# Weight transfers from ScalarE's queue, decay rows inside SBUF and two other edits at the start of an attention and two-layer feed-forward kernel

## The chip, the core and the metric

The kernel runs on one core of a Trainium2 chip. The metric is the device time of one execution in microseconds (us), the median of three runs. Engines are called as in the profile: PE (TensorE matmul), PEld (TensorE weight load), DVE (VectorE), ACT (ScalarE), POOL (GpSimd), SP (SyncE, which here only issues DMAs).

## What is computed

Causal attention with a forget-gate decay, then two feed-forward layers on the same 2304 tokens. Cut to its core:

```python
# batch 4, heads 8, seq 576, head_dim 64
scores  = q @ k.T / sqrt(64)
cum     = cumsum(log(clip(f, 1e-4, 1)))          # per batch and head
scores  = where(causal, -1e9, scores + cum[i] - cum[j])
attn    = softmax(scores)
x       = attn @ v                               # 2304 x 512
h = x @ w_in;  x = (h * tanh(softplus(h))) @ w_out            # d_ff 2048
x = (sigmoid(x @ w_gate) * (x @ w_val)) @ w_out2              # d_ff 1536
```

## The kernel before

**Stages.** Attention runs per batch (b = 0 to 3) and pair of heads (p = 0 to 3), in chunks of 128 query rows: chunks 0 and 1 are the first part of a batch, chunks 2, 3 and 4 the second. The first feed-forward layer works on blocks of 256 tokens (`h_ps`, then `y_ps`), eight groups g of 256 hidden units each; the second layer (`bank`, `o_acc`) follows. Each matrix is held as a sum of two float16 parts, so each product takes three matmuls. Attention of batches 1 to 3 is interleaved with the first layer; batch 0's first part has nothing beside it and opens the program.

**The order.** The kernel writes its instructions through a list scheduler of its own, the class `Order`. Every step is a task that yields an engine and an estimated duration (`yield "DVE", t_dve(512), "port"`); the scheduler keeps a clock for each engine and picks by due time and by readiness. The word "port" (or engine POOL) makes a step take a common clock that it keeps for DVE and POOL. `pick` chooses the engine of a step by the estimates. The estimates therefore decide both the order on each engine and who does what; on the chip each engine then runs its own list in that order, waiting on semaphores. Where `Order` sees PE idle for over 0.6 us it calls `fill`, which issues matmuls on the mask into the open accumulator before its first real use, or as products with zeros: work with no result (lines with `y_ps<-mask`, L1069).

**The start.** `decay` (L439) loads the gates `f` into `ft`, clips them (DVE, L447), takes the logarithm with its sum (ACT, L449), adds the carries of the four segments by a matmul (PE, L455, `carry_ps`) and scans (DVE, L460) into `cum`. `cum` is written to the DRAM scratch `cum_f` (L463), and from there `first_rows` (L525) brings it back as one row of `Q32` and one of `K32` (L533: keys rq, rk for the first 256 positions, rk2 for the rest). `Q32` (tile `sab`) and `K32` (tile `mab`) hold q and k in float32 with two more rows, so that one matmul gives scores plus decay; the constant rows are set on POOL by `ones` (L402). `prep_first` loads q and k (L544, L546).

**The first softmax.** `scores_first` (L734) makes two score tiles for chunks 0 and 1 of a pair (L741, `s_ps`), then in the same task, one after the other, the masked minimum on DVE (L698, helper `softmax_part`) and the exponential on ACT (L764); then the transposes by matmul (L788, `t_ps`), and `pv` multiplies with v (L952, `o_ps`).

**Weights.** `load_w` brings a weight piece of 512 KB as 64-bit numbers (L655, raw tile `xt`), turns it into float32 by three DVE steps (`float32`, L632, L636, L640) and splits it (`scaled` L495 on ACT, L498 on DVE; `rest` L514 on DVE, or L519 on ACT and L523 on POOL). Three raw buffers and two float32 buffers are in turn use. The first piece was held until the last q and k transfer was issued, the second until rk had landed; all are issued from SP. w_in needs 16 pieces and w_out 16.

Of the kernel before, what the change touches and what calls it, by code (L numbers as in the profile page):

```python
# [295 lines left out]

def t_dve2(cols):
    return cols * 0.52e-3 + 0.066
# [11 lines left out]
def attention_moe_moe_kernel(ctx, tc, qk, v, f, carry, ident, rows_q, rows_k, w_in, w_out, w_gate, w_val, w_out2, out):  # L310
# [121 lines left out]
    def decay():  # L432
        ft = words(xt[0], 1280, 2 * SL).bitcast(FP32)
        cum = words(xt[0], 1280 + 2 * SL, 2 * SL).bitcast(FP32)
# [26 lines left out]
        for seg in range(4):  # L461
            yield "SP", 0.5, 5000, ("cum_f", seg)
            nc.sync.dma_start(out=cum_f[:, seg * SL:(seg + 1) * SL], in_=cum[seg * NH:seg * NH + 2 * NPB])  # L463
            if seg == 1:
                spawn(first_rows(), -50)
                od.due(-20)
        yield from need(*[("cum_f", seg) for seg in range(4)])
# [32 lines left out]
    def rest(dst, a, scale, b, n, pool=False):  # L500
# [3 lines left out]
        plans = [[("DVE", t_dve(n), "port")]]  # L504
# [20 lines left out]
    def first_rows():  # L525
        yield from need("ones", ("cum_f", 0), ("cum_f", 1))
        for key, row, n in (("rq", Q32[64:65], 256), ("rk", K32[65:KF], 256), ("rk2", K32[65:KF], S)):
            c0 = 256 if key == "rk2" else 0
            if c0:
                od.due(-20)  # L530
                yield from need(("cum_f", 2), ("cum_f", 3))
            yield "SP", 0.5, 10000, key
            nc.sync.dma_start(  # L533
                out=row.rearrange("o a q s -> o (a q) s")[:, :, c0:n], in_=cum_f[:, c0:n].unsqueeze(0)
            )

    def prep_first(p, part, turn):
# [10 lines left out]
        if part:  # L548
            yield from need(("cum_f", 2), ("cum_f", 3))
# [5 lines left out]
        yield from need(*(("rk2", ("rq2", p)) if part else ("rq", "rk")))  # L555
# [47 lines left out]
    def prep_v(b, p, turn):  # L603
        i = b * NPB + p
        if b == 0:
            yield from need("rk")
# [14 lines left out]
        yield from scaled(t[:, :, 0, :], s, S_V, 640)  # L621
        yield from rest(t[:, :, 1, :], s, S_V, t[:, :, 0, :], 640, b < VPOOL)
# [7 lines left out]
    def float32(w, raw):  # L630
        yield "DVE", 0.335, "port"
# [3 lines left out]
        yield "DVE", 0.6, "port"  # L635
# [3 lines left out]
        yield "DVE", 0.6, "port"  # L639
# [4 lines left out]
    def load_w(hi, lo, src, scale, key, n):  # L644

        yield from need(*(((("st", NPB - 1),),) + (("rk",),) * n)[n])
# [5 lines left out]
        if n < NFIRST:  # L652
            od.due(-26.5)
# [277 lines left out]
    def pv(b, p, part, dues, turn):  # L931
# [41 lines left out]
        if cs[-1] == 4:  # L973
            give("vt", vi)
# [671 lines left out]
```

## Time and profile before

| | |
|---|---|
| median of 3 runs | 940.15 us (939.47 to 943.29) |
| the profiled execution | 940.69 us |
| its span, first to last instruction | 938.8 us |
| around the span | 1.89 us |
| mean granted TensorE clock | 0.987 |

PE is busy for 97% of the span, but a part of that is work on the mask, and a part runs at a lower clock. The views used below are the page's first two parts (busy time by engine, and the span in 40 slices), the table of windows (busy time of each engine in stretches of the span), the timeline of the first 25 us, and the timelines of POOL and DVE around 92 us.

### The profile page before, as it was taken

What the parts mean: (1) busy time and instruction counts of PE and PEld (TensorE: products, weight loads), DVE (VectorE), ACT (ScalarE), POOL (GpSimd) and SP (SyncE); (2) the same over time, 40 slices, a digit from 0 to 9 for tenths busy, and PEclk for the clock granted to TensorE, in tenths of its full rate; (3) what the DMA queues carried; (4) which work ended last, traced back from release to release, by engine and by line L of the source; (5) the groups of instructions that cost most, each with busy time, mean ns of one, the idle gap of its engine ahead of it and who ended that gap; (6) DMA issues with size and microseconds to landing.
All of it is one profiled execution on the core that took longest, in us unless ns stands there. A gap on an engine that the chain in (4) does not pass through costs nothing.

```text
span 938.8 us, 21014 instructions
## 1 busy us (share of the span) xinstructions
PE 910.6 (97%) x8619; PEld 718.0 (76%) x8619; DVE 589.6 (63%) x1348; ACT 559.5 (60%) x1097; POOL 84.6 (9%) x80
## 2 busy tenths in 40 slices
PE   6998999999999999999999999999999999999998
PEld 5656688778888888788888877777777777777786
DVE  5779989875765746666699999954136232432333
ACT  4788769888888878788444465544324332432343
POOL 3022302020111001000200010200000000000000
PEclk9879899999999999999999999999999999999999
DMA  6487997667465565635334443101000000100000
GB/s 194 125 208 196 226 229 198 142 128 150 113 141 117 110 148 107 124 66 93 100 121 151 157 134 115 45 6 41 1 1 23 24 1 1 45 1 1 12 36 23
DMA packets 145405, 90.47 MB, mean 96 GB/s; under 512 B 103599, under 2 KB 127119, under 8 KB 145310
## 3 DMA queue, kind: packets, MB, share of 16 engines
q1 hardware_dynamic: 145310, 89.15, 39.1%
q8 instruction: 67, 1.10, 0.5%
q14 instruction: 28, 0.23, 0.1%
HBM read 50.78 MB, written 4.85 MB: 59 GB/s over the span
## 4 chain that ended last, share of the span: by engine, by line
PE 42%; DVE 12%; DMA 2%; issue 1%; ACT 1%; POOL 1%; POOLq 0%; DVEq 0%; ACTq 0%
PE bank L1342 7%; PE bank L1343 7%; PE bank L1344 7%; PE o_acc L1490 4%; PE o_acc L1489 4%; PE o_acc L1488 4%; DVE wf L636 2%; DVE wf L640 2%; DMA wraw<-w_val 1%; DVE wf L632 1%; PE y_ps L1104 1%; PE o_ps L964 1%; DMA wraw<-w_gate 1%; DVE g L1027 1%; PE h_ps L1054 1%
## 5 line engine op out<-in xcount | busy, mean ns | idle before, releaser
L1054 PE MATMUL h_ps<-xt,win 128*128 128x256 f16 x576 | 158.2, 275 | 2.1 <-DVE g L1027 2.1
L1056 PE MATMUL h_ps<-xt,win 128*128 128x256 f16 x576 | 157.7, 274 | 2.3 <-POOL win L523 1.9
L1104 PE MATMUL y_ps<-g,wout 128*128 128x256 f16 x576 | 158.1, 274 | 0.1
L1055 PE MATMUL h_ps<-xt,win 128*128 128x256 f16 x576 | 157.8, 274 | 0.0
L1106 PE MATMUL y_ps<-g,wout 128*128 128x256 f16 x576 | 157.7, 274 | 0.0
L1105 PE MATMUL y_ps<-g,wout 128*128 128x256 f16 x576 | 157.7, 274 | 0.0
L1432 DVE TENSOR_TENSOR v<-bank,e 128x512 f32<-128x512 f32 (+1 forms) x30 | 19.1, 637 | 167.8 <-ACT bank L1349 167.8
L1349 ACT ACTIVATE bank<-bank 128x512 f32<-128x512 f32 (+1 forms) x90 | 48.5, 539 | 90.7 <-PE bank L1344 88.7
L514 DVE SCALAR_TENSOR_TENSOR pp<-sp,sm,pp 128x384 f16<-128x384 f32 (+4 forms) x120 | 77.7, 659 | 20.4 <-ACT pp L495 18.7
L698 DVE CUSTOM_DVE_ANT_0 sp<-s_ps,mask 128x384 f32<-128x384 f32 (+4 forms) x144 | 67.4, 492 | 30.3 <-PE s_ps L832 28.2
L495 ACT ACTIVATE pp<-sp,sm 128x384 f16<-128x384 f32 (+4 forms) x115 | 67.8, 606 | 9.9 <-issue 3.4
L847 ACT ACTIVATE sp<-sp,sm 128x384 f32<-128x384 f32 (+3 forms) x112 | 63.6, 569 | 13.3 <-DVE sm L698 12.5
L1054 PEld LDWEIGHTS <-win 128*128 128x128 f16 x576 | 56.6, 98 | 14.8 <-issue 3.2
L1055 PEld LDWEIGHTS <-win 128*128 128x128 f16 x576 | 56.7, 98 | 13.7 <-issue 5.1
L1104 PEld LDWEIGHTS <-wout 128*128 128x128 f16 x576 | 56.6, 98 | 11.0 <-ACT sp L910 0.9
L1056 PEld LDWEIGHTS <-win 128*128 128x128 f16 x576 | 56.6, 98 | 10.1 <-POOL win L523 2.2
L1105 PEld LDWEIGHTS <-wout 128*128 128x128 f16 x576 | 56.7, 98 | 7.8 <-issue 0.3
L1106 PEld LDWEIGHTS <-wout 128*128 128x128 f16 x576 | 56.6, 98 | 6.8
L1027 DVE SCALAR_TENSOR_TENSOR g<-h_ps,g 128x512 f16<-128x512 f32 x72 | 48.9, 684 | 19.1 <-ACT g L1023 18.8
L964 PEld LDWEIGHTS <-vt 128*64 128x64 f16 x1368 | 36.3, 112 | 15.2 <-issue 11.4
L1017 ACT ACTIVATE h_ps<-h_ps 128x512 f32<-128x512 f32 x72 | 41.7, 585 | 10.1 <-PE h_ps L1056 9.6
L964 PE MATMUL o_ps<-pt,vt 128*64 128x128 f16 (+1 forms) x1368 | 44.3, 216 | 2.7 <-DMA pt<-pp 1.6
(206 smaller groups left out, 2289.4 us busy)
## 6 DMA issues: line engine op xcount, KB each, us to landing
xt<-w_in SPq DMA_DIRECT2D x16, 512.0 KB
xt<-w_out SPq DMA_DIRECT2D x16, 512.0 KB
wraw<-w_gate SPq DMA_DIRECT2D x12, 512.0 KB
wraw<-w_val SPq DMA_DIRECT2D x12, 512.0 KB
wraw<-w_out SPq DMA_DIRECT2D x12, 512.0 KB
out<-ob SPq DMA_DIRECT2D x18, 256.0 KB
vst<-v SPq DMA_DIRECT2D x12, 320.0 KB
st<-qk SPq DMA_DIRECT2D x12, 320.0 KB
```

The costliest lines, as they stand in the source:

```text
L495: nc.scalar.activation(out=dst, in_=src, func=ACTF.Copy, scale=scale, bias=bias)
L514: nc.vector.scalar_tensor_tensor(dst, a, scale, b, op0=ALU.mult, op1=ALU.subtract)
L698: nc.vector.tensor_tensor_reduce(out=sp, in0=ps_ap, in1=mk, op0=ALU.add, op1=ALU.min, scale=-0.125, scalar=1.0e38, accum_out=mn,)
L964: nc.tensor.matmul(o_ps[64 * hh:64 * hh + 64, col:col + n], lhsT=vv[:, jc, vl, 64 * hh:64 * hh + 64], rhs=ptt[:, k, q0:q0 + n], start=(jc ...
L1054: nc.tensor.matmul(dst, lhsT=wh, rhs=xh, start=(k == 0), stop=False)
L1055: nc.tensor.matmul(dst, lhsT=wh, rhs=xl, start=False, stop=False)
L1056: nc.tensor.matmul(dst, lhsT=wl, rhs=xh, start=False, stop=(k == KD - 1))
L1104: nc.tensor.matmul(dst, lhsT=wh, rhs=gh, start=first, stop=False, skip_group_check=True)
L1105: nc.tensor.matmul(dst, lhsT=wl, rhs=gh, start=False, stop=False, skip_group_check=True)
L1106: nc.tensor.matmul(dst, lhsT=wh, rhs=gl, start=False, stop=last, skip_group_check=True)
L1342: nc.tensor.matmul(dst, lhsT=wh, rhs=xh[:, k], start=first, stop=False, skip_group_check=True)
L1343: nc.tensor.matmul(dst, lhsT=wh, rhs=xl[:, k], start=False, stop=False, skip_group_check=True)
```

## The change

The change does six things.

1. The first two weight pieces are issued from ACT's queue, the first before anything else there, the second when pair 0's q and k have been asked for (`NFIRST` = 2). All others stay on SP.
2. The constant rows of `Q32` and `K32` come by two DMAs from a new input `const`; the two POOL memsets go.
3. `cum` and `ft` lie in other tiles (`wout`), and the rows rq and rk go directly from `cum` in SBUF to their places, as two DMAs each; only segments 1 to 3 still go to `cum_f`, for the second part.
4. In `scores_first` the softmax of each chunk is a task of its own, `soft`, spawned as soon as its score tile is done, instead of a loop after both.
5. The estimates of DVE steps marked "port" become 0.049 us longer (`t_dvep`), those in `float32` 0.04 to 0.055 us.
6. The low part of v for batch 0 waits for that batch's last product (`("pv", i)`).

```diff
+def t_dvep(cols):
+    return cols * 1.04e-3 + 0.115
...
     def ones():
-        yield "POOL", 2.5
-        nc.gpsimd.memset(K32[64:KF], 8.0)
-        yield "POOL", 1.5
-        nc.gpsimd.memset(Q32[64:KF], -8.0)
+        yield "SP", 0.5, 10000, "ones_k"
+        nc.sync.dma_start(out=K32[64:65].rearrange("o a q s -> o (a q s)"), in_=const[0:1])
+        yield "SP", 0.5, 10000, "ones_q"
+        nc.sync.dma_start(
+            out=Q32[65:KF].rearrange("o a q s -> o (a q s)"), in_=const[1:2, 0:2 * NPB * 320]
+        )
+        yield from need("ones_k", "ones_q")
...
-        ft = words(xt[0], 1280, 2 * SL).bitcast(FP32)
-        cum = words(xt[0], 1280 + 2 * SL, 2 * SL).bitcast(FP32)
+        ft = words(wout[NG1 - 1], 1536, 2 * SL).bitcast(FP32)
+        cum = words(wout[NG1 - 2], 1536, 2 * SL).bitcast(FP32)
...
-        for seg in range(4):
+        for row, key in ((Q32[64:65], "rq"), (K32[65:KF], "rk")):
+            for seg in range(2):
+                n = min(SL, 256 - seg * SL)
+                yield "SP", 0.5, 10000, (key, seg)
+                nc.sync.dma_start(
+                    out=row.rearrange("o a q s -> o (a q) s")[:, :, seg * SL:seg * SL + n],
+                    in_=cum[seg * NH:seg * NH + 2 * NPB, 0:n],
+                )
+        od.due(-20)
+        for seg in range(1, 4):
...
-        plans = [[("DVE", t_dve(n), "port")]]
+        plans = [[("DVE", t_dvep(n), "port")]]
...
         yield from scaled(t[:, :, 0, :], s, S_V, 640)
+        if b == 0:
+            yield from need(("pv", i))
...
-        yield "DVE", 0.335, "port"
+        yield "DVE", 0.39, "port"
...
-        yield "DVE", 0.6, "port"
+        yield "DVE", 0.64, "port"
...
-        yield from need(*(((("st", NPB - 1),),) + (("rk",),) * n)[n])
+        if n:
+            yield from need(("st", 0) if n < NFIRST else ("rk", 1))
...
-            od.due(-26.5)
+            od.due(-40 + 9.9 * n)
         yield "SP", 0.5, 128 * 4096
-        nc.sync.dma_start(
+        (nc.scalar if n < NFIRST else nc.sync).dma_start(
...
+        def soft(gi, pst, tag, si):
+            c, n = gi, (gi + 1) * 128
+            yield from need("mask")
+            yield "DVE", 2 * t_dve(n)
+            for hh in range(2):
+                k = 2 * gi + hh
+                softmax_part(
+                    pst[:, hh * n:hh * n + n], mask[:, 512 - 128 * c:640], sps[k][1], sm[:, k:k + 1],
+                )
+            give(tag, si)
+            yield "ACT", 2 * t_act(n, 0.28), "exp"
...
-            banks.append((pst, tag, si))
+            spawn(soft(gi, pst, tag, si), od.cur["due"])
         give("q", qi)
-        for gi in range(2):
...
+        yield from need(("soft", p, 0), ("soft", p, 1))
         yield from weigh(sm, 4)
```

The new lines shift the line numbers: L632, L636 and L640 become L645, L649 and L653; L698 becomes L712; L455 becomes L462; L655 becomes L669.

**First place: the issuing queues at the start of the program.** SP before, from the second transfer on (`carry` and `ident` are constants; `mab` and `sab` are K32 and Q32):

```order
L442 DMA wout_84<-carry 128x128
L544 DMA mab<-qk 64x2x256
L546 DMA sab<-qk 64x2x256
L397 DMA win_83<-ident 128x128
...
L463 DMA cum_f<-xt_71 8x144 x2
L546 DMA sab<-qk 64x2x256
L544 DMA mab<-qk 64x2x256
L546 DMA sab<-qk 64x2x256
L533 DMA sab<-cum_f 1x8x256
L533 DMA mab<-cum_f 1x8x256
L655 DMA xt_74<-w_in 128x2x512
```

SP after, from the same transfer on (`wout_90` is `cum`):

```order
L449 DMA wout_84<-carry 128x128
L409 DMA mab<-const 1x4608
L411 DMA sab<-const 1x2560
L554 DMA mab<-qk 64x2x256
L556 DMA sab<-qk 64x2x256
L401 DMA win_83<-ident 128x128
L473 DMA sab<-wout_90 1x8x144
L473 DMA sab<-wout_90 1x8x112
L473 DMA mab<-wout_90 1x8x144
L473 DMA mab<-wout_90 1x8x112
L554 DMA mab<-qk 64x2x256
```

ACT after, its first rows (before, the queue began with the table load and held no transfer):

```order
L669 DMA xt_74<-w_in 128x2x512
L456 ACT_TABLE_LOAD
L456 ACTIVATE wout_91,wout_84<-wout_91 128x144
L457 ACT_TABLE_LOAD
L457 ACTIVATE wout_84<-wout_84 128x1
L669 DMA xt_73<-w_in 128x2x512
L510 ACTIVATE win_76<-xt_75 128x512
L763 ACTIVATE wout_88,sm<-wout_88,sm 128x128 x2
```

The rows of rq and rk now leave SP directly behind pair 0's q and k and ident, ahead of the q and k of pairs 1 to 3, and two weight transfers stand on ACT. With the semaphores shown, ident waits for the semaphore that the first weight transfer raises, and the transfer behind the four rows (pair 1's k) for that of the second.

**Second place: DVE, from the carry to the first softmax.** Before (`carry_ps` is the carry, `wout_88` pair 0's scores):

```order
L457 COPY wout_84<-carry_ps 128x1
L460 SCALAR_TENSOR_TENSOR xt_71<-xt_71,wout_84 128x144
L419 MEMSET mask_93 128x144
L420 COPY mask_93<-mask 64x64
...
L698 ISA wout_88,sm<-s_ps,mask 128x128
L698 ISA sm 128x1
...
L632 TENSOR_SCALAR xt_75<-xt_74 128x512
L471 CAST win_82<-xt_71 128x144
```

After:

```order
L464 COPY wout_84<-carry_ps 128x1
L467 SCALAR_TENSOR_TENSOR wout_90<-wout_91,wout_84 128x144
L645 TENSOR_SCALAR xt_75<-xt_74 128x512
L649 SCALAR_TENSOR_TENSOR xt_75<-xt_74,xt_75 128x512
L653 SCALAR_TENSOR_TENSOR xt_75<-xt_74,xt_75 128x512
L529 SCALAR_TENSOR_TENSOR win_76<-xt_75,win_76 128x512
L645 TENSOR_SCALAR xt_75<-xt_73 128x512
L649 SCALAR_TENSOR_TENSOR xt_75<-xt_73,xt_75 128x512
L712 ISA wout_88,sm<-s_ps,mask 128x128
```

Six steps of weight conversion moved from behind the first softmax to ahead of it. On PE, 18 of the mask matmuls now stand ahead of the carry and 14 between it and the first scores, where 35 stood behind the carry; in the whole program there are 138 of them, and 143 before. The engines' shares move too: POOL has 22 more two-input steps (`TENSOR_TENSOR`) than before.

## Rows read from the trace of the kernel before

**Rows 1.** The page's first two parts: busy us by engine; TensorE's granted clock, 40 slices.

```profile
PE 910.6 (97%) x8619; PEld 718.0 (76%) x8619; DVE 589.6 (63%) x1348; ACT 559.5 (60%) x1097; POOL 84.6 (9%) x80
PEclk9879899999999999999999999999999999999999
```

**Rows 2.** Windows: stretch, its us, busy us (and count) of each engine, PEclk, DMA, GB/s.

```profile
10.00:20.00 10.00, 7.41 (x52) 5.79 (x49) 5.70 (x29) 3.88 (x16) 0.00 (x0) 1.00 0.82 265
20.00:30.00 10.00, 9.31 (x43) 7.04 (x44) 8.37 (x31) 8.51 (x33) 0.00 (x0) 0.66 1.01 245
...
40.00:50.00 10.00, 9.46 (x59) 6.45 (x60) 9.90 (x30) 7.96 (x18) 0.44 (x1) 1.00 0.45 90
...
60.00:70.00 10.00, 10.00 (x65) 5.81 (x64) 8.35 (x23) 6.41 (x14) 0.00 (x0) 0.52 0.61 152
70.00:80.00 10.00, 9.09 (x72) 6.09 (x70) 9.86 (x23) 9.94 (x19) 0.69 (x1) 0.97 0.66 162
80.00:100.00 20.00, 16.30 (x152) 11.70 (x151) 19.68 (x46) 14.27 (x25) 5.44 (x6) 0.86 0.89 213
...
200.00:300.00 100.00, 100.00 (x1149) 83.80 (x1147) 64.61 (x193) 85.03 (x169) 12.60 (x13) 1.00 0.62 132
...
500.00:600.00 100.00, 98.70 (x826) 80.61 (x825) 92.70 (x157) 51.91 (x89) 10.81 (x6) 1.00 0.40 129
```

**Rows 3.** Timeline, 0 to 13 us: start, us, engine, line, step [idle before, releaser].

```profile
0.73 3.93 POOL L405 MEMSET mab<- 2x4608 f32 x1 [0.29 <-POOLq L1636]
2.67 2.08 DVE L447 TENSOR_SCALAR xt<-xt 128x144 f32<-128x144 f32 x1 [1.65 <-DMA xt<-f]
4.79 0.32 ACT L449 ACTIVATE xt<-xt 128x144 f32<-128x144 f32 x1 [2.78 <-DVE xt L447]
5.26 0.59 PE L455 MATMUL carry_ps<-wout 128*128 128x1 f32 x2 [5.26 <-ACT xt L449]
5.71 5.63 PE L1069 MATMUL y_ps<-mask 128*128 128x256 bf16 x35
6.15 0.52 DVE L460 TENSOR_TENSOR_SCAN xt<-xt,wout 128x144 f32<-128x144 f32 x1
6.70 0.67 SPq L463 DMA_DIRECT2D cum_f<-xt  x2
10.19 0.63 SPq L533 DMA_DIRECT2D mab<-cum_f  x1
12.35 1.55 PE L741 MATMUL s_ps<-mab,sab 66*128 66x128 f32 x8 [1.01 <-DMA mab<-cum_f]
```

**Rows 4.** Timeline, 5 to 25 us: table load, first weight piece, its steps, a softmax.

```profile
5.22 1.28 ACT L450 ACT_TABLE_LOAD   x1
10.86 0.45 SPq L655 DMA_DIRECT2D xt<-w_in  x1
13.06 0.29 DVE L698 CUSTOM_DVE_ANT_0 wout<-s_ps,mask 128x128 f32<-128x128 f32 x1 [4.66 <-PE s_ps L741]
14.60 0.43 DVE L632 TENSOR_SCALAR xt<-xt 128x512 int32<-128x512 int32 x1 [1.02 <-DMA xt<-w_in]
18.14 0.69 DVE L640 SCALAR_TENSOR_TENSOR xt<-xt,xt 128x512 int32<-128x512 int32 x1
```

**Rows 5.** PE's timeline, 30 to 110 us: first layer's first matmul, two longest waits.

```profile
41.51 0.27 PE L1054 MATMUL h_ps<-xt,win 128*128 128x256 f16 x1
...
58.88 0.28 PE L1056 MATMUL h_ps<-xt,win 128*128 128x256 f16 x1 [1.89 <-POOL win L523]
...
95.85 2.19 PE L894 MATMUL s_ps<-mab,sab 66*64 66x288 f32 x8 [2.71 <-DVE sm L698]
```

**Rows 6.** POOL's timeline, then DVE's, around 92 us.

```profile
92.03 1.30 POOL L523 TENSOR_TENSOR pp<-sp,pp 128x512 f16<-128x512 f32 x1 [6.96 <-ACT sp L519]
92.24 1.65 DVE L636 SCALAR_TENSOR_TENSOR xt<-xt,xt 128x512 int32<-128x512 int32 x1
98.17 0.67 DVE L636 SCALAR_TENSOR_TENSOR xt<-xt,xt 128x512 int32<-128x512 int32 x1
```

More of the change, by code (lines that the diff above doesn't have):

```diff
@@ L460, in decay @@
         nc.vector.tensor_tensor_scan(out=cum, data0=ft, data1=zt, initial=car, op0=ALU.add, op1=ALU.add)
-        for seg in range(4):
+        for row, key in ((Q32[64:65], "rq"), (K32[65:KF], "rk")):
[8 more added lines that the diff above has]
+        for seg in range(1, 4):
             yield "SP", 0.5, 5000, ("cum_f", seg)
             nc.sync.dma_start(out=cum_f[:, seg * SL:(seg + 1) * SL], in_=cum[seg * NH:seg * NH + 2 * NPB])
[L464 to L467, printed above, removed]
+        spawn(first_rows(), -20)
+        yield from need(*[("cum_f", seg) for seg in range(1, 4)])
         od.due(0)
@@ L525, in first_rows @@
     def first_rows():
[L526 to L532, printed above, removed]
-            nc.sync.dma_start(
-                out=row.rearrange("o a q s -> o (a q) s")[:, :, c0:n], in_=cum_f[:, c0:n].unsqueeze(0)
-            )
+        yield from need(*[("cum_f", seg) for seg in range(1, 4)])
+        yield "SP", 0.5, 10000, "rk2"
+        nc.sync.dma_start(
+            out=K32[65:KF].rearrange("o a q s -> o (a q) s")[:, :, 256:S], in_=cum_f[:, 256:S].unsqueeze(0)
+        )
     def prep_first(p, part, turn):
@@ L548, in prep_first @@
         if part:
-            yield from need(("cum_f", 2), ("cum_f", 3))
+            yield from need(*[("cum_f", seg) for seg in range(1, 4)])
             yield "SP", 0.5, 10000, ("rq2", p)
@@ L554, in prep_first @@
         yield from need(("k32", p, part), ("q32", p, part))
-        yield from need(*(("rk2", ("rq2", p)) if part else ("rq", "rk")))
+        first = [(k, seg) for k in ("rq", "rk") for seg in range(2)]
+        yield from need("ones", *(("rk2", ("rq2", p)) if part else first))
         done(("q", p, part))
@@ L605, in prep_v @@
         if b == 0:
-            yield from need("rk")
+            yield from need(("rk", 1))
             (vi,) = yield from take("vt", turn=turn)
@@ L638, in float32 @@
         )
-        yield "DVE", 0.6, "port"
+        yield "DVE", 0.64, "port"
         nc.vector.scalar_tensor_tensor(
@@ L974, in pv @@
             give("vt", vi)
+        done(("pv", i))
         t0 = b * S + cs[0] * 128
@@ L1158, in add @@
     def add(out, a, b, op, n):
-        (plan,) = pick([("DVE", t_dve(n), "port")], [("POOL", t_pool(n))])
+        (plan,) = pick([("DVE", t_dvep(n), "port")], [("POOL", t_pool(n))])
         yield plan
@@ L1260, in mixed @@
     def mixed(out, v, other):
-        yield "DVE", t_dve(512), "port"
+        yield "DVE", t_dvep(512), "port"
         nc.vector.scalar_tensor_tensor(out, v, S_VL / S_GT, other, op0=ALU.mult, op1=ALU.subtract)
@@ L1322, in s_pair @@
         yield from scaled(dst[:, 0], a, 1.0, n, pool=False)
-        yield "DVE", t_dve(n), "port"
+        yield "DVE", t_dvep(n), "port"
         nc.vector.tensor_tensor(dst[:, 1], a, dst[:, 0], op=ALU.subtract)
```

40 lines of the change are left out of this document (14 added, 26 removed).

## The prediction

> **What bounds the kernel now.** I read the page's busy times first: PE is busy for 97% of the span [rows 1]. The matmuls that count are the same in both kernels, so the time can only change through what else fills PE: waits, mask matmuls, and stretches at the lower clock. The windows then show where these are [rows 2]. From 200 us on PE is full at clock 1.00 and DVE has a third of its time free; there the end is set by PE's work alone, and a microsecond won before it arrives at the end. Before 100 us DVE is full: 9.90 of 10 us from 40 on, 9.86 of 10 from 70, 19.68 of 20 from 80, while PE waits for it; the longest wait there, 2.71 us, ends on a DVE step [rows 5]. Only from 10 to 20 us does DVE stand idle for long, 5.70 of 10 [rows 2]; before its first softmax at 13.06 it sat idle for 4.66 us [rows 4]. So the change is worth what it gives DVE earlier: work in the idle time at the start, or less work before 100 us.
>
> The start is one chain [rows 3]: gates land at 2.67, clip until 4.75, logarithm, carry at 5.26, scan until 6.67, row to DRAM at 6.70, row back until its wait ends at 12.35 with the first scores.
>
> **The change part by part.** The sum is made against the profiled execution, 940.69 us with a span of 938.8; it lies 0.54 above the median of 940.15, which I take off at the end.
>
> *Clip and carry.* The clip took 2.08 us for 144 columns and ended when the POOL memset that began at 0.73 for 3.93 us ended, at 4.66 [rows 3]. A one-input step of 512 columns takes 0.43 [rows 4], so without the memset the clip should take some 0.23 (my estimate from that row, scaled down with a fixed part): 1.85 us less. But the mask matmuls that now stand ahead of the carry take part of it back. 35 took 5.63 us, 0.161 each [rows 3], so 18 take 2.9 us. They need the mask memset, which now opens POOL at 0.73 and, with 640 columns at the old memset's 3.93 / 4608 us each, should be done by about 1.4; PE reaches the carry at 4.3 to 4.5 instead of 5.26. The carry to the scan's end took 6.67 - 5.26 = 1.41 us. The scan ends at about 5.8: **0.9 us** won, between 0.3 (mask matmuls at a lower clock, or gates late) and 1.8 (none of that).
>
> *Two hops become one.* From the scan's end to the first scores went 12.35 - 6.67 = 5.68 us: a write to DRAM, its landing, two row reads, their landing. The read of rk was issued at 10.19 and let PE go at 12.35, so issue and landing of one such transfer take 2.16 us [rows 3]. Now four transfers follow each other on SP; the two small writes took 0.67 together, a row read 0.63 [rows 3]. The last is issued 1.0 to 1.9 us after the scan and lands 2.16 later: 3.2 to 4.1 us in place of 5.68. How long a move inside SBUF from eight partitions into one takes is not in this trace; the nearest row is the read of rk, and I take it. Won **2.0 us** (1.6 to 2.5; nothing, if such a move needs what both hops did). The constant rows are cheap to issue, two transfers of some 0.6 ahead of pair 0's q and k, and finished long before the scan. First scores near 9.4 in place of 12.35, a gain of **2.9 us** from these two items.
>
> *Weights from ACT.* The issue of one takes 0.45, and 14.60 - 10.86 = 3.74 us pass until DVE can begin on it [rows 4]. The first now goes at 0.73 and is there at about 4.5, before the scan ends; the second waits for the logarithm and a table load of 1.28 [rows 4], goes at about 5 and lands near 9. On ACT the two issues delay nothing that is not waiting anyway: the logarithm waited for the clip for 2.78 us [rows 3]. Three steps and the low part of the first piece, and two steps of the second, cost DVE some 0.43 + 0.69 + 0.69 + 0.69 + 0.43 + 0.69 = 3.6 us (0.43 for a one-input step, 0.69 for a two-input one) [rows 4]. Before, they ran from 14.60 on, between the softmaxes, now from 5.8 to about 10, in time that was idle. They do not give 3.6 at the end: before 38 us DVE waits for other things too. Counting through DVE's list to the fourth pair's attention result (the fourth step on `xt<-o_ps`), one piece more has been turned into float32 than before: 0.43 + 2 x 0.69 = 1.8 us of work that DVE need not do when it is full. Half of it I count as arriving, **0.9 us** (0 to 1.8).
>
> From 10 to 20 us, where the first weight pieces moved before, the DMA engines were busy for 0.82 of the time at 265 GB/s [rows 2]; from 0.7 to 5 us, gates, carry and pair 0's q and k will now move beside 512 KB. The page "DMA: Bandwidth & Descriptors" of the Trainium skill (section "Issuing engines are not separate DMA queues") speaks against the edit: transfers issued from several engines run on the same 16 DMA engines and interleave, so that another queue saves only the time of issuing. By it ACT's queue would be worth two issues of 0.45, and the gates would land later. The gain counted above comes from the earlier date and not from the queue, and the gates may be 0.8 us late before the 18 mask matmuls no longer hide it.
>
> *A task per chunk.* The first chunk's softmax may run and free its score bank before the second is scored. DVE's work per pair is the same, and DVE is what PE waits for there, so I count nothing; at best a wait of PE for a bank goes, and the mask matmuls or the next wait for DVE take its place.
>
> *Estimates and the order.* Longer "port" steps make the scheduler move work off DVE. Counted step by step with the durations of the trace, DVE has some 3 us less to do by the first layer's tenth step, and ACT some 3 more, with 9.94 of 10 us busy from 70 on [rows 2]. And 22 more two-input steps go to POOL. One such step of 1.30 us at 92.03 made a DVE step that began at 92.24 take 1.65 instead of 0.67 [rows 6], so each may cost DVE up to 0.98. Some four of them fall before 100 us. I take **0.7 us** won (from 3 won to 4 lost).
>
> *Mask matmuls.* 138 for 143. A matmul of the span takes 910.6 / 8619 = 0.106 us in the mean [rows 1], 5 of them **0.5 us**.
>
> *The v task and the new `cum_f` order.* The second part's rows come from segments 1 to 3 to DRAM and back as before, now behind the transfers of v, and the second part's scores stand behind all first scores on PE, which cover it. Nothing, or 1 us lost if those scores come so early that the rows are late.
>
> Sum: 2.9 + 0.9 + 0.7 + 0.5 = 5.0. The profiled execution would take 935.7, the median **935.2 us**.
>
> **The rivals.**
>
> *A. The start is held by the second weight transfer.* DVE's list now has two steps of the second piece ahead of the first softmax. If that piece lands late, all softmaxes are queued behind it, and PE and ACT wait for them. It goes from ACT only after the logarithm and a table load, and pair 1's k waits on SP for the same landing. It would have to land at 12 instead of 9 for the first softmax to come at 13.1 as before. Then the 2.9 is lost and the rest stays: 940.15 - 0.9 - 0.7 - 0.5 = 938.0. For it: 512 KB from 0.73 on have company. Against: the 3.74 us were measured in a stretch with 265 GB/s of other traffic and weights together [rows 2].
>
> *B. Lower clock goes with the waits.* From 20 to 30 us the granted clock was 0.66 and from 60 to 70 it was 0.52, that is mostly the lower of the two levels (1.2 of 2.4 GHz); the second fell after PE's wait of 1.89 us that ended at 58.88, a wait for POOL's part of a weight piece [rows 2, 5]. A stretch like that costs 10 x 0.48 = 4.8 us of matmul time. If the earlier weights remove this wait, about as much again is won: 930.4. Against: such waits come from POOL's late steps, and POOL gets more of them; and PE now idles from the last of the 14 mask matmuls, near 7, to 9.4, which may lower the clock at the first scores.
>
> *C. POOL takes DVE's time: slower.* The 22 added POOL steps at up to 0.98 us make up to 21.6 us of DVE time [rows 6]. After 200 us DVE has room, except from 500 to 600, where it is busy for 92.70 of 100 [rows 2] and where four of the added steps lie in the second layer's weights. From ten hits at places where PE waits for DVE, the forecast's gain is used up and 4.8 more is lost: 935.2 + 9.8 = 945.0. The page "SBUF — State Buffer" of the Trainium skill (section "Who interferes with whom") says that a vector step with two SBUF inputs contends with a GpSimd step that reads SBUF and that the later one blocks fully; the trace agrees with 1.65 against 0.67, and by that rule no part of a hit is softened. Against C: most hits fall where PE has other work queued.
>
> **How the numbers follow.** Chances: forecast 0.48 (932.5 to 938), A 0.22, B 0.18, C 0.12. "Faster" means below 935.45, 0.5% under 940.15, about what a measurement can tell from no change. Of the forecast's 0.48 some 0.28 lie below it; with B that is 0.46. The rest of the forecast and A give 0.42 for no change, C gives 0.12 for slower. The forecast lies close to that border, which is why both are near even. For 8 in 10 the range takes the forecast, A and half of B, with the nearer part of C: 930.0 to 943.5.
>
> **What would show it.** The clip takes under 0.4 us and the scan ends near 5.8; if it ends after 6.5, the carry item is wrong. The first scores begin between 8.5 and 10.3; later means that the rows inside SBUF or rival A decide, told apart by what ended PE's or DVE's wait. DVE converts from 6 to 10 us, and its first softmax stands near 10. The first `h_ps` matmul comes at 37 to 38 in place of 41.51 [rows 5]. From 200 us on PE should be full as before; if the gap to the kernel before changes there, C or chance in the order decides. A granted clock of 1.00 from 60 to 70 speaks for B, DVE steps of 1.3 us and more beside POOL steps for C.

## The result and the profile after

The changed kernel takes **950.08 us** (median, 949.41 to 952.25) against 941.64 of the kernel before in the same session: a ratio of 1.0101, 95% interval 1.0079 to 1.0122. I had forecast 935.2 with 930.0 to 943.5; it became slower, by 1.0%. The profiled execution after took 952.25 us with a span of 950.5.

The page's busy times and granted clock of the changed kernel, beside [rows 1]:

```profile
PE 918.9 (97%) x8614; PEld 721.4 (76%) x8614; DVE 590.7 (62%) x1324; ACT 571.1 (60%) x1116; POOL 101.8 (11%) x100
PEclk7979999989989999999999999999999999999999
```

ACT has 11.6 us more and POOL 17.2 more, as expected of the estimates, but DVE is not relieved, with 24 instructions fewer. Its start on the timeline, beside [rows 3] and [rows 4] (start, us, engine, line, step, and in brackets the idle time before and what ended it):

```profile
1.42 3.84 PE L1084 MATMUL y_ps<-mask 128*128 128x256 bf16 x18 [1.42 <-POOL mask L419]
3.62 0.23 DVE L454 TENSOR_SCALAR wout<-wout 128x144 f32<-128x144 f32 x1 [1.23 <-DMA wout<-f]
4.12 0.19 ACT L456 ACTIVATION_READ_ACCUMULATOR wout<-wout 128x1 f32 x1
5.36 0.35 PE L462 MATMUL carry_ps<-wout 128*128 128x1 f32 x2
5.58 1.69 PE L1084 MATMUL y_ps<-mask 128*128 128x256 bf16 x14
6.01 0.52 DVE L467 TENSOR_TENSOR_SCAN wout<-wout,wout 128x144 f32<-128x144 f32 x1
9.96 1.35 PE L776 MATMUL s_ps<-mab,sab 66*128 66x128 f32 x6 [2.69 <-issue]
10.68 0.29 DVE L712 CUSTOM_DVE_ANT_0 wout<-s_ps,mask 128x128 f32<-128x128 f32 x1
38.12 0.27 PE L1069 MATMUL h_ps<-xt,win 128*128 128x256 f16 x1
```

The mask matmuls have two paces. In the kernel before the first 16 follow each other every 0.213 us and the rest every 0.109; the changed kernel has its first 16 at the slow pace too (before in two stretches that share a matmul, then after):

```profile
5.71 3.55 PE L1069 MATMUL y_ps<-mask 128*128 128x256 bf16 x16
8.86 2.47 PE L1069 MATMUL y_ps<-mask 128*128 128x256 bf16 x20
1.42 3.60 PE L1084 MATMUL y_ps<-mask 128*128 128x256 bf16 x16 [1.42 <-POOL mask L419]
```

The first scores come 2.39 us earlier, the first layer's first matmul 3.39 us earlier (41.51 before). Then the windows of the changed kernel, beside [rows 2] (stretch, its length, busy us and count of PE, PEld, DVE, ACT, POOL, then granted clock, DMA share, GB/s):

```profile
0.00:100.00 100.00, 86.85 (x640) 61.43 (x640) 75.54 (x204) 72.59 (x164) 14.72 (x18) 0.86 0.68 181
...
10.00:20.00 10.00, 8.64 (x31) 6.41 (x31) 5.63 (x29) 6.25 (x25) 0.91 (x1) 0.59 0.78 226
...
60.00:70.00 10.00, 7.66 (x51) 4.62 (x49) 7.67 (x20) 7.54 (x14) 1.07 (x1) 0.66 0.68 180
...
180.00:190.00 10.00, 3.65 (x21) 1.67 (x19) 8.50 (x25) 6.54 (x16) 1.55 (x2) 0.79 0.62 123
190.00:200.00 10.00, 8.00 (x76) 4.92 (x76) 5.59 (x17) 7.62 (x17) 2.60 (x3) 0.53 0.69 143
200.00:300.00 100.00, 96.60 (x1079) 80.06 (x1078) 60.45 (x178) 81.09 (x162) 13.79 (x14) 0.97 0.61 118
```

and the same of the kernel before, which its rows ahead did not show:

```profile
0.00:100.00 100.00, 83.58 (x635) 59.31 (x636) 78.68 (x214) 71.91 (x163) 18.28 (x18) 0.89 0.71 181
...
180.00:190.00 10.00, 10.00 (x111) 7.94 (x108) 8.53 (x26) 9.51 (x22) 2.60 (x3) 1.00 0.60 125
190.00:200.00 10.00, 7.90 (x125) 5.94 (x123) 7.28 (x24) 8.47 (x17) 0.93 (x2) 1.00 0.83 163
```

In the first 100 us PE is busy for 3.3 us more, but at a clock of 0.86 in place of 0.89, some 3 us of full speed, so that little of the early start is left: the 97th `h_ps` matmul stands at 73.9 us, before at 73.5. The 385th stands at 169.0, before at 173.1, but in another order, so that this is no lead of the whole work. Then comes **the loss**: from 180 to 190 PE has work for 3.65 of 10 us, and after that it runs mostly at the lower of its two levels (0.53, that is near 1.2 of 2.4 GHz). PE's timeline there:

```profile
185.72 1.30 PE L908 MATMUL s_ps<-mab,sab 128*64 128x288 f16 x8 [4.17 <-DVE sm L712]
188.03 0.48 PE L845 MATMUL s_ps<-mab,sab 128*128 128x384 f16 x1 [1.00 <-DVE sm L712]
...
190.34 1.17 PE L978 MATMUL o_ps<-pt,vt 128*64 128x128 f16 x18 [1.51 <-DMA pt<-pp]
...
194.77 1.17 PE L978 MATMUL o_ps<-pt,vt 128*64 128x128 f16 x18 [1.66 <-DVE xt L1004]
...
196.70 0.42 PE L1069 MATMUL h_ps<-xt,win 128*128 128x256 f16 x1
```

At 196.70 begins the 394th `h_ps` matmul; before, it stood at 186.37. Blocks 0 and 1 take 384 of them; the next nine, of block 2, need the first three pairs of batch 1's first part, and the 394th is the first that needs the fourth. All 777 feed-forward matmuls that can run ahead of that (393 `h_ps`, 384 `y_ps`) had been used up by 180.7, and PE had only attention left, whose steps wait for each other through four engines. The longest wait, 4.17 us, ends on DVE, which from 179.1 us on had low parts (L529) and sums and splits of the first layer (L1142, L1151) ahead of that softmax. I call the eviction of the fourth pair's result (from `o_ps` to `xt`, by ACT and then DVE) **X15**: it ends at 184.3 before and 194.7 after. The chain of waits up to it, from the view that follows the last work back (start, us, what):

```profile
184.73 1.46 SPq L885
...
186.29 1.77 SPq L885
...
188.12 3.69 DMA st<-qk
...
191.89 0.06 ACT mab L510
...
192.43 0.77 ACT pp L510
...
193.22 0.77 ACT sp L534
193.99 0.28 ACT xt L1001
...
194.29 0.44 DVE xt L1004
...
194.77 1.17 PE o_ps L978 x17
```

Two transposes were issued on SP, a later batch's `st<-qk` behind them; ACT's queue stood still for that transfer for 1.23 us, until 191.89, and X15's eviction (ACT L1001) was queued behind its conversion and behind two passes for a low part. It began at 193.90, 2.4 us after PE had finished the product at 191.51.

There is a second place. From 200 to 300 us PE has one wait, near 262 us, and after it the granted clock falls again (the line of the table of waits gives total us, times, longest; then the window):

```profile
PE h_ps L1069 <- DVE g L1042: 3.3, 1, 3.3
```

```profile
260.00:270.00 10.00, 6.71 (x56) 4.96 (x55) 5.34 (x13) 8.77 (x18) 1.40 (x1) 0.72 0.66 132
```

### The profile page after: what moved, and what is told of

It is laid out like the page before. It is cut to its first block, busy times and chain, and to the rows that moved or that the text cites. A ratio compares the mean times of both kernels' runs of the same rounds, so it can differ in the third digit from the quotient of the medians.

```text
span 950.5 us, 21037 instructions
## 1 busy us (share of the span) xinstructions
PE 918.9 (97%) x8614; PEld 721.4 (76%) x8614; DVE 590.7 (62%) x1324; ACT 571.1 (60%) x1116; POOL 101.8 (11%) x100
## 3 DMA queue, kind: packets, MB, share of 16 engines
q1 hardware_dynamic: 144786, 88.12, 38.3%
## 4 chain that ended last, share of the span: by engine, by line
PE 70%; DVE 5%; ACT 3%; DMA 2%; SPq 1%; issue 1%; POOL 0%; POOLq 0%; ACTq 0%
PE bank L1357 8%; PE bank L1359 8%; PE bank L1358 8%; PE h_ps L1069 5%; PE h_ps L1071 5%; PE h_ps L1070 5%; PE y_ps L1119 5%; PE y_ps L1120 5%; PE y_ps L1121 5%; PE o_acc L1505 4%; PE o_acc L1504 4%; PE o_acc L1503 4%; PE o_ps L978 3%; PE s_ps L845 1%; PE s_ps L846 1%; DMA wraw<-w_val 1%
## 5 line engine op out<-in xcount | busy, mean ns | idle before, releaser
L529 DVE SCALAR_TENSOR_TENSOR pp<-sp,sm,pp 128x384 f16<-128x384 f32 (+4 forms) x113 | 74.3, 669 | 23.4 <-ACT pp L510 22.6
L712 DVE CUSTOM_DVE_ANT_0 sp<-s_ps,mask 128x384 f32<-128x384 f32 (+4 forms) x144 | 67.4, 493 | 28.5 <-PE s_ps L846 23.9
L978 PEld LDWEIGHTS <-vt 128*64 128x64 f16 x1368 | 38.5, 117 | 17.9 <-issue 12.9
L978 PE MATMUL o_ps<-pt,vt 128*64 128x128 f16 (+1 forms) x1368 | 46.9, 222 | 3.9 <-DMA pt<-pp 2.0
```

The lines of the kernel that those rows point to most:

```text
L529: nc.vector.scalar_tensor_tensor(dst, a, scale, b, op0=ALU.mult, op1=ALU.subtract)
L978: nc.tensor.matmul(o_ps[64 * hh:64 * hh + 64, col:col + n], lhsT=vv[:, jc, vl, 64 * hh:64 * hh + 64], rhs=ptt[:, k, q0:q0 + n], start=(jc ...
```

## The experiments

**Theories.** T1: the new estimates move work from DVE to ACT and POOL, and those bound batch 1's attention. T2: the earlier start makes the feed-forward run ahead. T3: any change of the order moves the time by some us, whatever its kind. T4 came later: the order decides by where it puts batch 1's attention among the feed-forward matmuls. Three of the orders (before, after, no_est) were also drawn a second time by a change that means nothing, the scheduler's window `NEAR`. Where an expectation names X13, its counts of feed-forward matmuls are those ahead of X15's product in the trace (708 forecast and 708 found in after_late00).

All kernels, with X15, the feed-forward matmuls that PE had done when X15's product ended (777 is all of them), and PE's idle time in three stretches (length less busy time, from the windows). Each ratio is against the kernel before in the same session, where its median lay between 940.2 and 942.2; across rows the ratios are the safer comparison:

| kernel | median, us | ratio to before (95%) | X15, us | ahead | 150-200 | 200-536 | 536-640 |
|---|---|---|---|---|---|---|---|
| before | 940.2 | 1 | 184.3 | 754 | 3.7 | 1.0 | 1.8 |
| after | 950.1 | 1.0079 to 1.0122 | 194.7 | 777 | 8.4 | 3.4 | 0.3 |
| est_only | 948.0 | 1.0053 to 1.0098 | 196.2 | 777 | 7.8 | 0.8 | 0.0 |
| no_est | 941.1 | 0.9978 to 1.0021 | 186.3 | 775 | 2.8 | 1.1 | 3.0 |
| before_near12 | 960.8 | 1.0185 to 1.0253 | 188.7 | 748 | 3.9 | 3.3 | 15.0 |
| after_near12 | 946.0 | 1.0038 to 1.0084 | 196.0 | 777 | 11.7 | 0.2 | 0.1 |
| no_pick | 936.9 | 0.9930 to 0.9975 | 187.4 | 777 | 6.2 | 0.2 | 0.0 |
| pick_only | 939.5 | 0.9952 to 0.9994 | 184.2 | 754 | 1.0 | 0.0 | 2.6 |
| before_dve | 946.1 | 1.0032 to 1.0061 | 189.7 | 777 | 7.5 | 0.4 | 3.8 |
| no_est_near12 | 959.4 | 1.0146 to 1.0213 | 182.6 | 777 | 8.3 | 2.5 | 15.2 |
| yield_only | 950.9 | 1.0062 to 1.0139 | 187.2 | 757 | 2.5 | 7.9 | 0.2 |
| pick_start | 946.9 | 1.0045 to 1.0082 | 180.2 | 748 | 1.1 | 0.8 | 9.2 |
| after_late00 | 935.4 | 0.9920 to 0.9959 | 178.9 | 708 | 1.9 | 0.0 | 0.0 |
| nopick_late00 | 938.8 | 0.9953 to 0.9997 | 177.9 | 724 | 2.5 | 2.0 | 0.0 |
| before_late00 | 937.3 | 0.9944 to 0.9978 | 182.1 | 753 | 3.4 | 0.0 | 0.8 |
| no_est_late00 | 943.5 | 0.9993 to 1.0052 | 175.3 | 691 | 3.3 | 4.5 | 1.1 |
| est_only_late00 | 948.6 | 1.0055 to 1.0106 | 188.9 | 777 | 6.1 | 2.7 | 0.0 |
| after_latem05 | 953.3 | 1.0103 to 1.0167 | 177.1 | 715 | 3.8 | 1.0 | 14.7 |

**The two halves of the change.** est_only is the kernel before with part 5 of the change alone, no_est the changed kernel without part 5.

```diff
 def t_dvep(cols):
-    return cols * 1.04e-3 + 0.115
+    return cols * 1.04e-3 + 0.066     # no_est; 0.39 and 0.64 back to 0.335 and 0.6
```

> The kernel before with VectorE's estimates alone (0.115 in place of 0.066 as the fixed part, 0.39 and 0.64 in the weight split); the start is the old one. T1, the estimates push work to ScalarE and GpSimd, and ScalarE bounds batch 1's attention: 945 to 955 us, ScalarE busy over 565 us (559.5 in the kernel before, 571.1 in the changed one), PE waiting 8 us or more between 150 and 200 us. T2, the earlier start makes the feed-forward steps run ahead of the attention and the estimates are harmless: 937 to 943. T3, any change of the order moves the time by some us whatever its kind: anywhere between 935 and 950, and the two kernels with another NEAR scatter as widely.

> The changed kernel with the old estimates. T1: 934 to 941 us, ScalarE busy about 560, no long wait of PE between 150 and 200 us. T2: 945 to 952, with PE waiting in 180 to 200 as in the changed kernel. T3: between 935 and 950.

Measured 948.0 and 941.1, ACT 571.1 and 559.0 us busy, X15 at 196.2 and 186.3. Both are as T1 said, or a hair outside (941.1 where it said up to 941, and PE idle for 7.8 us from 150 to 200 where it said 8 or more); T3 allowed both as well. T2 falls, since the start alone doesn't make PE run dry. But the start alone didn't make the kernel faster either, though its first `h_ps` matmul came at 37.8.

**A second draw of the order.**

```diff
-NEAR = 0.1
+NEAR = 0.12
```

> The kernel before with NEAR, the planner's window for what counts as ready at once, 0.12 in place of 0.1: another order, nothing else meant. T1 and T2: within 3 us of the kernel before. T3: 4 us or more away from it, in either direction.

> The changed kernel with NEAR 0.12 in place of 0.1. T1: ScalarE busy over 565 us still, and the time 945 us or more. T2: as T1, if the feed-forward steps run ahead here too. T3: 4 us or more away from 950, most likely downwards, since one draw that was bad is followed by a middling one.

The kernel before went to 960.8, 20 us away with nothing changed in its meaning, as only T3 allowed; the changed kernel to 946.0, as T1 and T3 both allowed. In before_near12 PE idles for 15.0 us between 536 and 640 us, 13.2 more than in the kernel before. Its waits there (line, releaser, total us, times, longest):

```profile
PE bank L1342 <- ACT bank L1349: 14.4, 3, 13.0
```

There the second layer's first products wait for an eviction on ACT. That eviction (L1349) began at 611.11. In PE's 13 us ACT had six conversions of the second layer's weights and sums (`wf`, `af`) ahead of it and waited for DVE before five of them; DVE was busy for 12.13 of the 13 us with steps of the same kind (the window, then ACT's last two steps):

```profile
598.70:611.70 13.00, 0.04 (x1) 0.00 (x0) 12.13 (x20) 4.25 (x8) 1.53 (x1) 0.61 0.01 2
610.58 0.63 ACT L495 ACTIVATE win<-af 128x512 f16<-128x512 f32 x1 [0.52 <-DVE af L1162]
611.11 0.58 ACT L1349 ACTIVATE bank<-bank 128x512 f32<-128x512 f32 x1
```

So ACT's order puts the eviction behind conversions that wait for DVE.

**Which of the estimates.** no_pick keeps the new durations, but chooses the engine of a low part (`rest`) and of an addition (`add`) by the old price; pick_only is the reverse, on the kernel before.

```diff
-        plans = [[("DVE", t_dvep(n), "port")]]
+        plans = [[("DVE", t_dve(n), "port")]]      # and in add; the step itself still counts t_dvep(n)
```

> The changed kernel, but the choice of an engine for a low part and for an addition is made with the old price of VectorE (0.066); all other new estimates stay. T1a, the new price in that choice is what costs, because each low part it takes from VectorE puts a pass on ScalarE and one of 1.2 us on GpSimd, beside which VectorE's steps run longer: 937 to 944 us, GpSimd busy about 85 and X15, the last evictions of batch 1's first part, by 188 us (194.7 in the changed kernel). T1b, the longer durations themselves move the order: still 945 or more. T3, the order alone: no relation.

> The kernel before with the new price (0.115) in that one choice alone. T1a: as with all the estimates alone, 945 to 950 us, ScalarE busy over 567, GpSimd over 100, X15 at 192 us or later (184.3 in the kernel before). T1b: within 3 us of the kernel before. T3: no relation.

no_pick: 936.9, as T1a said. pick_only: 939.5, with X15 at 184.2 and this on its page, POOL busier than in the changed kernel:

```profile
PE 908.6 (97%) x8629; PEld 716.7 (76%) x8629; DVE 584.9 (62%) x1329; ACT 563.9 (60%) x1109; POOL 110.5 (12%) x101
```

That is against T1a: the extra work on POOL is there, and the kernel is not slower for it. no_pick shows too that the hole alone doesn't set the time: all 777 matmuls stand ahead of X15, PE idles for 6.2 us from 150 to 200, and it is the second fastest kernel.

**No low part on POOL.**

```diff
-        plan = pick(*plans[1 if pool else 0:])
+        plan = pick(*plans[0:1])
```

> The kernel before with every low part on VectorE: none is shared with ScalarE and GpSimd. T1a in its strong form, that a low part on GpSimd takes from VectorE as much as it gives: VectorE's busy time stays within 8 us of 589.6 although it has some 30 steps more, and the time is within 4 us of 940 or below. If GpSimd really relieves VectorE: VectorE busy over 605 and the time 945 to 960, with PE waiting more before 100 us.

946.1 with 598.2 us of DVE: 38 more instructions and 8.6 us more, 0.23 us each, about a third of the 0.67 of a two-input step of 512 columns [rows 6]. One pair of orders is thin for that, but a straight line through the 18 orders of the table, DVE's busy time against its number of instructions, gives 0.19 (standard error 0.04). So POOL does relieve DVE, by much less than a step. The strong form of T1a falls, by 0.6 us of DVE time and by 2 us of the median; the other forecast, DVE over 605, missed too.

> The changed kernel with the old estimates and NEAR 0.12: a second draw of the order for the new start. T1: X15 by 189 us and 936 to 944 us. T3: anywhere between 935 and 960, as the kernel before went from 940 to 961 with NEAR 0.12.

959.4 with X15 at 182.6: T1 missed it. As in before_near12 the loss lies between 536 and 640 us, 15.2 us.

**The two missing corners.** yield_only: old start, new durations, old choice. pick_start: new start, old durations, new choice.

> The kernel before with the new durations of VectorE's steps, but the choice of an engine at the old price: the one corner that is missing with the old start. T1, the extra work on ScalarE and GpSimd is what delays batch 1: 938 to 943 us, since no low part moves. T4, the order alone decides, by how many feed-forward matmuls it puts ahead of batch 1's last evictions (754 ahead of X15 in the kernel before, all 777 in the changed one): here some 750, so 938 to 944 and X15 by 188 us. T3, a draw: anywhere between 935 and 960.

> The changed kernel with the old durations, but the choice of an engine at the new price: the missing corner with the new start. T1: ScalarE busy over 567 us, GpSimd over 100, and 945 to 950 us. T4: the order puts some 747 feed-forward matmuls ahead of X13 where the changed kernel puts 777: X15 by 188 us and 936 to 942 us. T3: a draw.

950.9 and 946.9. T1's range held for pick_start, though ACT was busy for 565.4 us and not over 567; it forecast 938 to 943 for yield_only and falls. Of the four combinations of durations and choice, the old start gives 940.2 (none), 939.5 (choice), 950.9 (durations), 948.0 (both), the new one 941.1, 946.9, 936.9, 950.1: each half is good with one start and bad with the other. That is no price of the work; these are orders. T4 missed both times as well: X15 came early (187.2, 180.2), as it said, and the time was lost elsewhere. In yield_only PE waited between 200 and 300 us, in the next part of the attention, this time for transposes most of all:

```profile
PE o_ps L968 <- DMA pt<-pp: 3.7, 3, 2.0
PE s_ps L898 <- DVE sm L702: 2.6, 1, 2.6
```

**Moving only the hole.** after_late00 is the changed kernel with the due times of batch 1's first attention half a step earlier; nothing else differs.

```diff
-    LATE = 0.5
+    LATE = 0.0
```

> The changed kernel with batch 1's first attention due half a step earlier (LATE 0 in place of 0.5), all estimates and start edits kept. T4: X13 now stands behind 708 feed-forward matmuls in place of 777, PE has feed-forward left while it waits for X15, the hole of 180 to 196 us is under 3 us, and the time is 937 to 943. T1: ScalarE and GpSimd have the same extra work, X15 stays at 193 or later, 946 or more. T3: a draw.

**935.4 us, 14.7 less than the changed kernel**, with ACT at 567.2 and POOL at 105.4, the extra work of the estimates. X15's eviction and the windows:

```profile
178.50 0.42 DVE L1004 SCALAR_TENSOR_TENSOR xt<-o_ps,xt 128x256 f16<-128x256 f32 x1
```

```profile
180.00:200.00 20.00, 20.00 (x235) 16.25 (x234) 14.37 (x41) 16.99 (x33) 3.69 (x5) 1.00 0.69 110
200.00:300.00 100.00, 100.00 (x1160) 83.44 (x1158) 63.02 (x194) 87.13 (x181) 18.19 (x19) 1.00 0.68 134
```

PE is full from 180 to 300 us at clock 1.00: the hole, the low clock behind it and the later waits are gone. T1 said 946 or more; T4 had the hole right and the time 1.6 us too long. It is the fastest kernel of all, ahead of both the kernel before and the changed one.

> The fastest so far (the changed kernel with the old price in the choice of an engine, 936.9) with the same half step. T4: PE's waits between 183 and 188 us, 5 us there, shrink: 932 to 937. T1 and T3: no gain, 936 or more.

938.8 (934.4 to 942.8): X15 at 177.9, but no gain, since 2.0 us went in the stretch from 200 us on. T4 missed.

**Is that one lucky draw?** The half step on the other three corners, and a whole step.

> The kernel before with batch 1's first attention due half a step earlier and nothing else. T4, the order decides and the start's gain arrives once PE has no hole: the kernel before lost only 3.7 us in that place, so 936 to 941 us, and 2 to 4 us behind the changed kernel with the same half step (935.4). T3, draws: anywhere between 935 and 960.

> The changed kernel with the old estimates and the half step. T4: X15 by 183 us, no hole over 3 us in 150 to 200, and 934 to 939 us; the start's gain is there without the estimates. T3: a draw.

> The kernel before with the new estimates and the half step. T4 by its order: X13 still stands behind all 777 feed-forward matmuls, as without the half step, so the hole stays: X15 at 190 or later and 943 to 950 us. If the half step itself helps whatever the order: 936 to 941. T3: a draw.

> The changed kernel with batch 1's first attention due a whole step earlier (LATE -0.5). T4: X13 behind 714 feed-forward matmuls, as with half a step (708): X15 by 183 us and 934 to 940 us. T3: a draw, and the 935.4 of the half step was luck.

before_late00: 937.3, inside T4's range. est_only_late00: 948.6 with 777 ahead of X15, as T4 said from its order, with X15 at 188.9 where it said 190 or later. no_est_late00: X15 at 175.3, yet 943.5, with 4.5 us lost from 200 to 536. after_latem05: X15 at 177.1, as T4 said, and 953.3, as only T3 allowed. It kept pace with after_late00 until 585 us and then waited:

```profile
PE bank L1357 <- ACT bank L1364: 11.7, 2, 11.3
PE bank L1357 <- DVE t L1453: 2.3, 2, 2.0
```

So T4 holds for the hole at X15: in the seven kernels whose X15 stands behind all 777 matmuls PE idles for 6.1 to 11.7 us from 150 to 200, in the eleven others for 1.0 to 3.9 (no_est, with 775, 2.8). It doesn't hold for the whole time, because there are two more places where the order can leave PE without work, and closing one redraws the others. Nor does the half step help as such: with the new start and all estimates it gave 14.7 us, with the old start 2.9, and on the three other corners nothing (the medians rose by 0.6 to 2.4); the whole step gave nothing either. What it did to the changed kernel is shown, that it would do so elsewhere is not.

**The worth of the start with the order kept.** Seven more scans of the gates, which the scheduler doesn't count: each engine's list is the same, instruction by instruction.

```diff
-        nc.vector.tensor_tensor_scan(out=cum, data0=ft, ...)
+        for _ in range(8): nc.vector.tensor_tensor_scan(out=cum, data0=ft, ...)
```

> The changed kernel with the scan of the gates done eight times in place of once (the same result), some 3.4 us on VectorE ahead of the decay rows and of its first softmax; the order on all engines is unchanged. If the start counts one for one: 953 to 954 us, X15 3 us later. If the hole before X15 is set by what is ahead of it from the start: the same. If what lies between absorbs the delay (VectorE and ScalarE have idle time from 100 us on): 949 to 951, X15 within 1 us of 194.7.

> The same seven further scans in the changed kernel with LATE 0 (935.4 us), where PE has no long hole after 180 us. If the start counts one for one when PE is full later: 938 to 939 us. If what lies between absorbs it: 935 to 936.5.

The scans took 4.39 us in place of 0.52, the first `h_ps` matmul came at 42.4 (38.1) and 43.0 (38.3). The medians rose from 950.1 to 953.6 and from 935.4 to 938.9, both by 3.5, ratios 1.0110 to 1.0158 and 0.9961 to 0.9998. The profiled executions rose by only 0.8 and 1.7 us; there X15 came 2.1 and 1.1 us later. One for one is the medians' answer. It is not exact: by the ratios, each against the kernel before of its own session, the two kernels lost 3.1 and 3.8 us, the intervals of the first pair overlap (1.0079 to 1.0122 and 1.0110 to 1.0158), and those of the second just touch (up to 0.9959, from 0.9961). That a delay of 3.9 us at the start costs something at the end is shown in the second, and that it costs all of it is not.

**Where the time lies.** All 20 traces can be added up in the same way: idle time of PE, half of its busy time at the lower level of the clock (what the full level would have saved), and 0.107 us for each mask matmul. What is left of the span is 881 to 885 us in every one of them, so the orders differ in these three terms and hardly in anything else. In us, worked out from the traces:

| traced execution | span | idle | lower level | mask matmuls | rest |
|---|---|---|---|---|---|
| before | 938.8 | 28.2 | 13.1 | 15.3 | 882.2 |
| after | 950.5 | 31.6 | 22.3 | 14.8 | 881.8 |
| no_est | 942.4 | 26.8 | 20.3 | 13.3 | 882.0 |
| after_late00 | 934.1 | 21.9 | 14.6 | 16.2 | 881.4 |

So the greater part of the loss is the clock: of 11.7 us between the two traces 9.2 are the lower level and 3.4 idle time. From 150 to 536 us the changed kernel has 7.1 us more of idle time, and it lost 7.6 at the lower level behind the two holes (from 185.8 to 199.5 and from 264.4 to 271.2), where the kernel before had none. The runs without a trace agree: the mean granted clock of all runs of the changed kernel is 0.978, and 0.991 to 0.992 for the kernel before, by session.

The start has a share of its own. From 10 to 25 us PE is granted 0.50 to 0.58 in all ten orders with the new start, and 0.84 to 1.00 in the eight with the old one (the kernels named before or est_only, with pick_only and yield_only). The rows are those of before, then no_est:

```profile
10.00:25.00 15.00, 11.73 (x71) 8.92 (x69) 10.37 (x50) 8.88 (x36) 0.00 (x0) 0.93 0.91 267
10.00:25.00 15.00, 14.45 (x50) 11.41 (x51) 9.44 (x46) 8.41 (x33) 0.73 (x1) 0.50 0.86 242
```

Ahead of its first scores PE idles for 1.9 to 2.7 us in the ten and for at most 1.2 in the eight. Over the first 100 us the ten idle 4.2 us less in the mean and have 2.0 less of mask matmuls, but lose 5.0 more at the lower level: 1.1 us of the early start is left at that point (standard error 0.8). no_est kept more, 3.4 us against the kernel before, and lost 6.7 between 100 and 200 us, 2.7 of them idle and 4.0 at the lower level. Which edit of the start brings the lower level from 10 to 25 us was not tried.

## Why the prediction was wrong

- **Clip.** Right in size (0.23 us), wrong in the sum. I gave the gates 0.8 us of slack and they landed 0.95 later than before (3.62 against 2.67 [rows 3]), but that cost nothing: the logarithm was done at 4.31. What held the carry were the 18 mask matmuls, which took 3.84 us, 0.213 each, where I had taken 0.161. That 0.161 was the mean of two paces, and all but the last two of the 18 run at the slow one. The carry stands at 5.36, the scan ends at 6.53 instead of 5.8, after the 6.5 that I had named as the sign of a wrong item: 0.14 us won where I counted 0.9, below my 0.3.
- **Two hops to one.** From the scan's end to the first scores 3.43 us, forecast 3.2 to 4.1: right, 2.25 us won. Together 2.39 against 2.9.
- **Weights from ACT.** DVE converted from 6.45 on, and the first softmax stood at 10.68, as said. The first `h_ps` matmul came at 38.12, a little behind the 37 to 38 of the forecast. The page "DMA: Bandwidth & Descriptors" of the Trainium skill (section "Issuing engines are not separate DMA queues") says that such transfers share the same engines. The gates' later landing agrees: 3.21 to 3.62 us in all ten orders with the new start, 2.59 to 2.73 in the eight with the old one. No run took this edit alone.
- **"A microsecond won before 100 us arrives at the end."** The held kernels go that way in their medians, with one condition that I left out: that the order stays. As an argument across two orders it failed. no_est had the whole start, 3.7 us early at the first `h_ps`, and ended at 941.1. Part of the reason is a term that I put at nothing: under rival B I noted that PE's idle time ahead of the first scores may lower the clock there, and gave it no price. In the mean it cost 5.0 us in the first 100, more than all that the start was forecast to bring (2.9 + 0.9 + 0.5). And a reading was wrong: the 5.70 of 10 us from 10 to 20 [rows 2] is DVE's busy time; it stood idle for 4.30.
- **"From 200 us on PE is full at clock 1.00"**, with which I set aside everything behind 200. That was a row of the kernel before [rows 2], and I read it as a property of the kernel, past another row there: from 500 to 600 PE was busy for 98.70 of 100 us and DVE for 92.70. It belongs to that order: among 18 orders of the same work PE idles from 0 to 8 us between 200 and 536, and from 0 to 15 between 536 and 640. The place where it broke in the changed kernel, 180 to 196 us, was full in the trace of before from 180 to 190; near it stood one wait of 2.10 us at 198.59, for another step. No row of before named the place, and the sum had no term for it.
- **"Estimates and the order: 0.7 won, from 3 won to 4 lost."** This is the step that failed by most. I costed the work that moved, step by step, and let the order itself be worth nothing more. The order of the changed kernel put all 777 feed-forward matmuls ahead of X15. That hole, the one near 262 us and the lower clock behind both cost 14.7 us against the kernel before, 7.1 idle and 7.6 at the lower level, and the medians give the same 14.7 back for a half step of due time. The 18 orders lie between 935.4 and 960.8 us, mean 945.7, standard deviation 7.4; the kernel before, at 940.2, is one of the better ones, with five faster and twelve slower by the medians. They are no random sample, but by them the term for a new order should have been some 5 us lost, give or take 7. That the loss came out at 9.9, and not at half or twice as much, was the luck of the draw.
- **Rivals.** A fell (the first softmax was not held). B fell as a gain: the clock was 0.66 from 60 to 70 and 0.59 from 10 to 20; the fear noted there, that PE's idle time ahead of the first scores lowers it, came true (2.69 us idle, then 0.59). C had the right sign and half the size (945.0), and its mechanism is in the trace: DVE's steps beside POOL took 37.5 us above the median of their own kind (counting those more than a tenth above it), 25.1 before. But it isn't what made the time: pick_only has 31.0 of that, more POOL work than the changed kernel, and 939.5 us.

What stays open: which edit of the start lowers the clock from 10 to 25 us, and how much of the early start is in after_late00, which can't be told from its order. Moving the late eviction between 536 and 640 us ahead of the weights on ACT was not tried.

## What to carry to other kernels

Where a scheduler orders the work, an edit of its inputs is a new draw: before any term of it is counted, draw the old kernel's order a few times with changes that mean nothing, and use that spread as the term's range. A view that says an engine is full holds for that order only; look instead for the hand-over points, where the work that can run runs out and a chain of other engines must have delivered. When such an edit loses, find the late chain and try its due time before giving up the edit: here that was worth 14.7 us. It is one more draw, though: of six such moves here two won and four didn't. And when work is moved earlier, price the idle time that it leaves on PE: here the lower clock behind it took back most of the gain.

## What the runs showed of the hardware

- A low part moved from DVE to POOL relieved DVE by about 0.2 us, of 0.67 for a step of 512 columns (598.2 - 589.6 us for 38 instructions; 0.19 by the line through 18 orders). The rest comes back as longer DVE steps beside POOL, like the 1.65 of [rows 6]: counted as under rival C, these took 25.1 us too long before and 9.4 in before_dve.
- The first 16 mask matmuls of 256 columns followed each other every 0.213 us in both kernels, the later ones every 0.109. The granted clock has no entry in the traces until that change of pace (9.1 us before, 4.9 after), so the 1.00 that the windows show ahead of it is no reading; the pace is that of the `h_ps` matmuls at the lower level, 0.21 us apart from 196.70 on, and half that of the later ones.
- After the wait of 4.17 us PE was granted the lower level from 185.8 to 199.5 us, and an `h_ps` matmul took 0.42 us in place of 0.27. After the wait of 3.3 us near 262 it was granted it from 264.4 to 271.2. Both holes cost more than their length: 7.6 us of PE's work on top of 7.1 more of idle time.
